# Attention beside an MLP on one core: where the products of softmax weights and values stand in the order of TensorE's work

## The chip, the core and the metric

The kernel runs on one core of a Trainium2 chip. The metric is the device time of one launch in microseconds (us), the median of three runs. The profile is one execution of the same program, recorded on the chip.

## The reference

```python
scores = (1 / sqrt(64)) * q @ k.T              # 8 batches, 8 heads, 576 positions, head size 64
scores = where(pos_q // 64 >= pos_k // 64, scores, -1e9)
attn   = softmax(scores)                       # less the row's maximum; the sum gets 1e-9 added
x      = attn @ v                              # heads side by side: x is 4608 x 512
out    = (sigmoid(x @ w_gate) * (x @ w_val)) @ w_out     # 512 -> 1536 -> 512
```

All of it is float32 at the outside.

## The kernel before

**Two halves.** The first half, about 550 us of the span, is the attention with a part of the MLP dealt in between. The second half is the rest of the MLP (lines 875 and 953), and the change does not reach its code. Where an operand is split into a high and a low fp32r part (names in H and L, such as `KH`, `KL`), a product is three matmuls: high by high, high by low, low by high.

**Pairs.** The attention goes over 32 pairs `p` of heads, four to a batch. Of a pair's 576 query rows, 512 are four blocks of 128 (3, 2, 1, 0); the last 64 rows of both heads are the tail. The steps of a pair, as the tables name them:

- `s`: scores of blocks 3, then 2, then 1 and 0 together (`s_blocks`, line 258, `bank<-KH,QH` and the like; block 0 is `bank<-KQ`). Per block VectorE masks (L409, L411), takes the maxima (L385), and ScalarE takes the exponentials into `P` (L388). The two heads lie in the upper and lower 64 rows of TensorE (64\*128).
- `t`: scores of the tail (`s_tail`; `QBH`, `QBL`), 128\*128; maxima L425, exponentials `Pt` L427.
- `r`: reciprocals of the row sums (L433 to L436), then two DMAs on SP's queue: to DRAM (`r_d`, L439) and back, spread over the partitions (`rb`, L442).
- `tr3`, `tr2`, `trl`, `trt`: transposes of the weights of block 3, block 2, blocks 1 and 0, and the tail, on TensorE (L262, `bank<-ident,P` and `bank<-ident,Pt`); ScalarE copies each result from PSUM into `G1` or `G0` (L363). The copy of `trt` (`128x8x64` and `128x2x64` in the order) puts the tail's columns beside those of the blocks in `G1`.
- `AV`: products of weights and values (`av`, `bank<-G,VS`, 128\*64: the heads lie in the left and right 64 columns). Its first matmul reads 320 columns of `G1`, the tail's 64 among them. VectorE multiplies the result by `rb` into `xT` (L507), ScalarE and GpSimd split `xT` for the MLP (L514, L519).
- `k`, `q`: the next pair's operands are prepared (VectorE transposes L290, casts L327, L328, L331, L332, GpSimd L336), and loads are issued on SP's queue.

**Order.** A table names the steps of a pair in their order with a number behind each: so many ticks, and in each tick some products of the MLP are dealt (`m`, lines 131 and 138: 128 by 512, full array). Pairs 0 to 7 have their own tables (`ALONE`, `FIRST`, `TURN`); pairs 8 to 31 use `REST`. `AV` in the row of pair p is that of pair p-1. A scheduler puts the instructions on the engines' queues; `behind(a, b)` keeps `a` behind `b`. In pairs 8 to 31 the first matmul of `s` and that of `AV` stand behind the product dealt last, and the last matmul of either is put into `hold`, behind which products dealt later and the transposes stand. A product may be dealt up to three ticks ahead of its place. A batch's MLP products are added to the supply with the `AV` of its last pair.

**PSUM.** The attention has three double banks in turn (`two_banks`, names `bank`), the MLP two single ones (`mbank`, names `m`). A step that takes a double bank waits until its last use has been read.

Of the kernel before, what the change touches and what calls it, by code (L numbers as in the profile page):

```python
# [30 lines left out]
         ("tr3", 1), ("r", 0), ("ld", 0))  # L31
ALONE = (("S3", 1), ("TR2", 1), ("k", 1), ("S2", 1), ("q", 1), ("m3", 0), ("m2", 0), ("TRt", 1), ("t", 1), ("TRl", 1), ("sl", 1), ("AV", 2),
         ("tr3", 1), ("r", 0), ("ld", 0))
REST = (("s", 3), ("t", 1), ("AV", 2), ("tr3", 1), ("r", 0), ("k", 0), ("tr2", 1), ("q", 0), ("trl", 2), ("trt", 2))
TURN = (("s3", 1), ("TR2", 1), ("k", 0), ("s2", 1), ("TRt", 1), ("q", 0), ("t", 1), ("TRl", 1), ("sl", 1), ("AV", 1),
        ("tr3", 1), ("r", 0), ("tr2", 1), ("trl", 1), ("trt", 1))
N_FIRST = 7
# [5 lines left out]
def attn_glu_kernel(ctx: ExitStack, tc: tile.TileContext, q, k, v, w_gate, w_val, w_out, out):  # L43
# [26 lines left out]
    def behind(ins, other):  # L70

        tc.add_manual_dep(ins, other.name, mybir.DependencyInfo(mybir.DependencyClass.NoSync,
                                                                mybir.DependencyReason.DATA), reason="order")
# [90 lines left out]
    with ExitStack() as s2:  # L164
# [78 lines left out]
        pe_last, first_mm, hold, dealt, chain = [], [], [], [], []  # L243
# [23 lines left out]
        def two_banks():  # L267
            return ps_a.tile([P, 2, 512], F32, name="bank")
# [80 lines left out]
        def attend(p):  # L349
# [10 lines left out]
            rest = p > N_FIRST  # L360
# [4 lines left out]
            def scores(ps, i, c):  # L365


                n = P * (i + 1)
                q = slice(i * P, (i + 1) * P)
                ops = [(KQ[:, 1, q], KQ[:, 0, :n])]  # L370
                if rest and i:
                    q = slice((i - 1) * P, i * P)
                    ops = [(QS[a][:, q], KS[b][:, :n]) for a, b in ((0, 0), (1, 0), (0, 1))]
                for k, (x, y) in enumerate(ops):
                    for h in range(2):
                        matmul(ps[:, h, c:c + n], lhsT=x[rows(h)], rhs=y[rows(h)], start=(k == 0),
                               stop=(k == len(ops) - 1), tile_position=(64 * h, 0))
                        if h == k == 0:
                            first_mm[:] = pe_last

            def softmax(ps, i, c):
                n = P * (i + 1)
                c0 = col[i]
                Pi = keep[i] = p_tile(i)
                mark("DVE", nc.vector.tensor_reduce(out=nm[:, c0:c0 + 2], in_=ps[:, :, c:c + n], axis=AX.X, op=ALU.max,  # L385
                                                    negate=True))
                for h in range(2):
                    mark("ACT", nc.scalar.activation(out=Pi[:, h], in_=ps[:, h, c:c + n], func=AF.Exp,  # L388
                                                     bias=nm[:, c0 + h:c0 + h + 1], accum_out=sm[:, 5 * h + i:5 * h + i + 1]))
                    if i == 3 and 0 < p < NP:  # L390
                        behind(last["ACT"], q_copied[-1])

            def s_blocks(*groups, alone=False):


                tiles = [two_banks() for _ in groups]
                for k, (ps, group) in enumerate(zip(tiles, groups)):
                    for j, i in enumerate(group):
                        scores(ps, i, 2 * P * j)
                        if rest and dealt and k == j == 0:  # L400
                            behind(first_mm[0], dealt[-1])
                if rest:
                    hold[:] = pe_last
                if alone:
                    yield
                for ps, group in zip(tiles, groups):
                    n = P * (group[0] + 1)
                    if len(group) == 1:
                        nc.vector.memset(ps[0:64, :, n - 64:n], -1e9)  # L409
                    else:  # L410
                        nc.vector.memset(ps[0:64, :, P:3 * P].rearrange("p h (i n) -> p h i n", i=2)[:, :, :, 64:], -1e9)  # L411
                    for j, i in enumerate(group):
                        softmax(ps, i, 2 * P * j)
# [109 lines left out]
            def step(what):  # L523
                if what in ("S3", "S2"):
                    soft[what] = s_blocks((int(what[1]),), alone=True)
                    next(soft[what])
                elif what in ("m3", "m2"):
                    run(soft.pop("S" + what[1]))
                elif what == "s":
                    run(s_blocks((3,), (2,), (1, 0)))  # L530
                elif what[0] == "s":
                    run(s_blocks({"s3": (3,), "s2": (2,), "sl": (1, 0)}[what]))
                elif what == "t":
                    s_tail()
                elif what == "r":
                    recip()
                elif what == "tr3":
                    tr_main(3)
                elif what == "tr2":
                    tr_main(2)  # L540
                elif what == "trl":
                    tr_low()
                elif what == "trt":
                    tr_tail()
                else:
                    av()
                    finish()
# [264 lines left out]
        for p in range(n + 1):  # L812
# [3 lines left out]
            tick = 0  # L816
            for what, places in (ALONE if p < NP else FIRST if p < N_FIRST else TURN if p == N_FIRST else REST):
                if what.startswith(("AV", "TR")):
# [17 lines left out]
                for _ in range(places if now else 6 if what == "AV" else 0):  # L836
                    pe_ticks.append(pe_last[0])
                    acc += rate
                    while acc >= 1:
                        acc -= 1  # L840
                        left -= 1
                        ins = next(mlp, None)
# [252 lines left out]
```

## Time and profile before

| | |
|---|---|
| median of 3 runs | 1180.55 us (1180.47 to 1180.87) |
| span of the profiled execution | 1177.6 us |
| TensorE (PE) busy | 1153.6 us, 98% |
| weight loads (PEld) | 976.3 us, 83% |
| VectorE (DVE) / ScalarE (ACT) / GpSimd (POOL) | 776.6 / 617.4 / 349.6 us |
| granted TensorE clock, mean | 0.995 |
| first scores of pair 8 / 13 / 31 | 125.67 / 220.17 / 527.61 us into the span |

The profile's page gives the span alone for its execution and no device time of its own; the median of the runs lies 2.95 us above that span. PE is TensorE's matmuls, PEld its weight loads. In a row of the timeline stand the start, the duration, the engine, the line, the operation with its output and inputs, and the count of instructions that were merged; the ends of matmuls are modelled and overlap the next one's start, so the step from start to start is what a matmul costs.

### The profile page before, as it was taken

How to read it: one execution, taken by the hardware profiler on the slowest of the kernel's cores; microseconds unless marked ns; L12 is line 12 of the kernel's file. 1: busy time of each engine (PE TensorE's matmuls, PEld its weight loads, DVE VectorE, ACT ScalarE, POOL GpSimd, SP SyncE). 2: the span in 40 equal slices, each digit the busy share in tenths (PEclk: the TensorE clock that was granted, in tenths of full speed). 3: DMA queues.
4: the chain of work that ended last, by engine and by line, in shares of the span. 5: the costliest groups of instructions: out<-in, count | busy, mean ns of one | idle time of the engine just before them, and what ended most of it. 6: DMA issues, size and time to landing. Idle time of an engine off the chain costs nothing.

```text
span 1177.6 us, 19283 instructions
## 1 busy us (share of the span) xinstructions
PE 1153.6 (98%) x6749; PEld 976.3 (83%) x6749; DVE 776.6 (66%) x1405; ACT 617.4 (52%) x1364; POOL 349.6 (30%) x390
## 2 busy tenths in 40 slices
PE   6999999999999999999999999999999999999998
PEld 4555778778777877787889899999999998998997
DVE  5778845454564555457959977867877746746754
ACT  5867766766676676666334443553453422423421
POOL 2345523222331322234002133032033263262330
PEclk8999999999999999999999999999999999999999
DMA  8765434435434443534323236235197455164241
GB/s 198 180 144 115 104 89 100 117 74 127 99 89 112 102 122 71 125 105 134 111 95 126 91 120 223 71 136 202 39 339 276 158 172 179 39 212 132 83 143 54
DMA packets 253361, 153.34 MB, mean 130 GB/s; under 512 B 193232, under 2 KB 215248, under 8 KB 252624
## 3 DMA queue, kind: packets, MB, share of 16 engines
q1 hardware_dynamic: 241600, 132.15, 40.1%
q10 hardware_dynamic: 11280, 18.91, 4.4%
q8 instruction: 53, 0.87, 0.3%
q0 software_dynamic: 384, 1.05, 0.3%
q14 instruction: 44, 0.36, 0.1%
HBM read 104.73 MB, written 47.33 MB: 129 GB/s over the span
## 4 chain that ended last, share of the span: by engine, by line
PE 90%; DVE 5%; ACT 2%; issue 1%; DMA 1%; POOL 0%; SPq 0%; DVEq 0%; ACTq 0%
PE b L875 27%; PE bank L258 14%; PE m L131 14%; PE m L953 11%; PE m L138 7%; PE bank L262 6%; PE b L953 5%; PE bank L131 3%; ACT P L388 1%; PE m L262 1%; PE bank L138 1%; DVE nm L385 1%; DVE XL L765 0%; DMA raw<-in_moe_w_out_dram 0%; DMA rqk<-in_k_dram 0%
## 5 line engine op out<-in xcount | busy, mean ns | idle before, releaser
L875 PE MATMUL b<-XH,w 128*128 128x384 f32 x1344 | 349.2, 335 | 1.2 <-DVE g L921 1.2
L875 PEld LDWEIGHTS b<-XH,w 128*128 128x128 f32 x1344 | 243.9, 188 | 5.2 <-DVE g L921 1.6
L875 PE MATMUL b<-XL,w 128*128 128x384 f32 x672 | 223.5, 335 | 0.0
L388 ACT ACTIVATE P<-bank,nm 128x512 f32<-128x512 f32 (+3 forms) x256 | 132.1, 530 | 68.3 <-DVE nm L385 68.2
L385 DVE TENSOR_REDUCE nm<-bank 128x2 f32<-128x1024 f32 (+3 forms) x128 | 105.4, 823 | 40.7 <-ACT P L388 37.6
L875 PEld LDWEIGHTS b<-XL,w 128*128 128x128 f32 x672 | 126.1, 188 | 1.6
L953 PE MATMUL m<-wo,hH 128*128 128x512 f32 x384 | 125.0, 391 | 0.0
L363 ACT COPY G<-bank 128x768 f32<-128x768 f32 (+3 forms) x140 | 93.2, 694 | 26.2 <-PE bank L262 25.3
L258 PE MATMUL bank<-G,VS 128*64 128x320 f32 (+4 forms) x896 | 93.9, 360 | 0.1
L751 POOL TENSOR_TENSOR XB<-XB 128x384 f32<-128x384 f32 x20 | 20.7, 1037 | 237.9 <-DMA XB<-xT_d 191.6
L138 PE MATMUL m<-wo,hH 128*128 128x512 f32 x256 | 85.4, 398 | 1.4 <-ACT ost L632 1.0
L258 PEld LDWEIGHTS bank<-G,VS 128*64 128x64 f32 x896 | 55.9, 137 | 36.7 <-issue 4.3
L900 ACT ACTIVATE g<-g 128x384 f32<-128x384 f32 x72 | 37.8, 526 | 88.5 <-DVE g L913 48.6
L953 PEld LDWEIGHTS m<-wo,hH 128*128 128x128 f32 x384 | 72.0, 188 | 13.5
L131 PE MATMUL m<-XH,wv 128*128 128x512 f32 x240 | 82.3, 400 | 0.0
L131 PE MATMUL m<-XH,wg 128*128 128x512 f32 x240 | 82.1, 399 | 0.0
L764 ACT CAST XH<-XB 128x1536 fp32r<-128x1536 f32 (+2 forms) x72 | 65.2, 941 | 29.4 <-DVE XB L762 24.1
L765 DVE TENSOR_TENSOR XL<-XB,XH 128x1536 fp32r<-128x1536 f32 (+2 forms) x72 | 75.8, 1084 | 0.0
L262 PEld LDWEIGHTS bank<-ident,P 128*128 128x128 f32 x560 | 65.8, 141 | 11.5 <-ACT P L388 0.8
L953 PE MATMUL m<-wo,hL 128*128 128x512 f32 x192 | 75.2, 392 | 0.0
L262 PE MATMUL bank<-ident,P 128*128 128x128 f32 x560 | 74.8, 273 | 0.1
L409 DVE MEMSET bank<- 64x128 f32 x64 | 10.6, 165 | 88.0 <-PE bank L258 87.3
(183 smaller groups left out, 2339.5 us busy)
## 6 DMA issues: line engine op xcount, KB each, us to landing
xT_d<-xT ACTq DMA_DIRECT2D x32, 288.0 KB
XB<-xT_d SPq DMA_DIRECT2D x16, 576.0 KB
part_d<-ost SPq DMA_DIRECT2D x36, 256.0 KB
VS<-in_v_dram SPq DMA_DIRECT2D x64, 128.0 KB
part_d<-ost ACTq DMA_DIRECT2D x32, 256.0 KB
rqk<-in_k_dram SPq DMA_DIRECT2D x108, 72.0 KB
rqk<-in_q_dram SPq DMA_DIRECT2D x108, 72.0 KB
wgv_d<-st SPq DMA_DIRECT2D x8, 896.0 KB
```

Of the source, the lines that this page charges most:

```text
L131: mm = nc.tensor.matmul(ps, lhsT=lh, rhs=rh, start=(i == 0), stop=(i == n - 1))
L138: mm = nc.tensor.matmul(ps, lhsT=lh[:, f, t * P:(t + 1) * P], rhs=rh, start=(f == i == 0), stop=(f == F1 - 1 and i == 2))
L258: pe_last[:] = [nc.tensor.matmul(*args, **kw).ins]
L262: pe_last[:] = [nc.tensor.transpose(*args).ins]
L363: mark("ACT", nc.scalar.copy(out=dst, in_=src))
L385: mark("DVE", nc.vector.tensor_reduce(out=nm[:, c0:c0 + 2], in_=ps[:, :, c:c + n], axis=AX.X, op=ALU.max, negate=True))
L388: mark("ACT", nc.scalar.activation(out=Pi[:, h], in_=ps[:, h, c:c + n], func=AF.Exp, bias=nm[:, c0 + h:c0 + h + 1], accum_out=sm[:, 5 * h ...
L764: nc.scalar.copy(out=XO[j][0][:, a:b], in_=x)
L765: sub = nc.vector.tensor_sub(out=XO[j][1][:, a:b], in0=x, in1=XO[j][0][:, a:b].bitcast(F32))
L875: mm = nc.tensor.matmul(ps, lhsT=lh, rhs=rh, start=(first and k == 0), stop=(k == n - 1), skip_group_check=not first)
L900: mark2("ACT", nc.scalar.activation(out=t, in_=c, func=AF.Tanh, scale=0.5))
L953: mm = nc.tensor.matmul(po[t], lhsT=lh[:, f, t * P:(t + 1) * P], rhs=rh, start=(half == 0 and i == 0), stop=(half == 1 and i == 5))
```

## The change

In `REST` the products of weights and values move from behind the tail's scores to the head of the row, with no tick between them and the scores of the pair. The ticks move too: four behind the scores instead of three, two behind the tail's scores instead of one, one behind `trl` instead of two, three behind `trt` instead of two; there are twelve as before. With `AV` the point at which a batch's products join the supply moves to the head of the pair. The first matmul of the scores is kept behind the product dealt last and behind `hold`, which is the last matmul of `AV` there.

```diff
-REST = (("s", 3), ("t", 1), ("AV", 2), ("tr3", 1), ("r", 0), ("k", 0), ("tr2", 1), ("q", 0), ("trl", 2), ("trt", 2))
+REST = (("AV", 0), ("s", 4), ("t", 2), ("tr3", 1), ("r", 0), ("k", 0), ("tr2", 1), ("q", 0), ("trl", 1), ("trt", 3))
...
                         scores(ps, i, 2 * P * j)
-                        if rest and dealt and k == j == 0:
-                            behind(first_mm[0], dealt[-1])
+                        if rest and k == j == 0:
+                            for ins in (*dealt, *hold):
+                                behind(first_mm[0], ins)
```

What this does to the queues is seen in the order of the built programs. In it `bank<-ident,Pt` are the tail's transposes, `bank<-G,VS` is `AV`, `bank<-KH,QH` the scores, `m<-` the MLP's products. A line number behind the diff is one higher after the change.

TensorE before, at the seam between two pairs (the end of pair 15, the start of pair 16):

```order
L131 MATMUL m<-XH_387,wv_113 128x512
L262 MATMUL bank<-ident,Pt 128x128 x5
L138 MATMUL m<-wo,hH 128x512
L138 MATMUL m<-wo,hL 128x512
L138 MATMUL m<-wo,hH 128x512 x2
L258 MATMUL bank<-KH,QH 128x512 x2
L258 MATMUL bank<-KH,QL 128x512 x2
```

Four products stand between the tail's transposes and the next scores.

TensorE before, in pair 16, where the tail's scores (`QBH`, `QBL`) end and `AV` of pair 15 stands:

```order
L258 MATMUL bank<-KL,QBH 128x288
L258 MATMUL bank<-G_2842,VS_94 64x320 x6
L258 MATMUL bank<-G_2842,VS_94 64x64 x2
L258 MATMUL bank<-G_2842,VS_94 64x192 x2
L258 MATMUL bank<-G_2843,VS_94 64x256 x2
L258 MATMUL bank<-G_2843,VS_94 64x128 x2
L138 MATMUL m<-wo,hL 128x512
```

`AV` stands between the tail's scores and MLP products, far behind the transposes that it reads.

TensorE now, at the same seam, between pairs 15 and 16:

```order
L138 MATMUL m<-wo,hH 128x512 x2
L138 MATMUL m<-wo,hL 128x512
L138 MATMUL m<-wo,hH 128x512
L262 MATMUL bank<-ident,Pt 128x128 x5
L258 MATMUL bank<-G_2861,VS_94 64x320 x6
L258 MATMUL bank<-G_2861,VS_94 64x64 x2
L258 MATMUL bank<-G_2861,VS_94 64x192 x2
L258 MATMUL bank<-G_2862,VS_94 64x256 x2
L258 MATMUL bank<-G_2862,VS_94 64x128 x2
L258 MATMUL bank<-KH,QH 128x512 x2
```

The tail's transposes, `AV` of the same pair and the scores of the next now stand one behind the other without a product between them.

ScalarE now, at the seam between pairs 19 and 20 (`G_3638` is the copy of `trl`, the two rows of `G_3637` that of `trt`, `ost` an MLP output):

```order
L328 ACTIVATE QH<-KQ 128x448
L363 COPY G_3638<-bank 128x768
L633 ACTIVATE ost<-m 128x512
L363 COPY G_3637<-bank 128x8x64
L363 COPY G_3637<-bank 128x2x64
L636 DMA part_d<-ost 128x512
L515 CAST XH_387<-xT 128x576
```

ScalarE copies the low blocks, then an MLP output, then the tail; the cast of `xT` (L515) now stands behind the tail's copies, ahead of the next pair's exponentials.

In full the order of TensorE's steps in a pair was `s` (20 matmuls), 12 products, `t`, `AV`, 6 products, `tr3`, 3, `tr2`, 3, `trl`, 8, `trt`, 4. Now it is `AV`, `s`, 20 products, `t`, `tr3`, 4, `tr2`, 9, `trl`, 3, `trt` (in every fourth pair 7 and 5 instead of 9 and 3). The seams behind pairs 8 to 11 still have 5 to 11 products between `trt` and `AV`; the 20 seams behind pairs 12 to 31 have none. Behind the last pair's `AV` follow 311 products instead of 323.

## The prediction

> **What bounds the kernel now.** I read the page first, then the stretch of the attention, then TensorE's timeline through one seam between two pairs.
>
> ```profile
> span 1177.6 us, 19283 instructions
> PE 1153.6 (98%) x6749; PEld 976.3 (83%) x6749; DVE 776.6 (66%) x1405; ACT 617.4 (52%) x1364; POOL 349.6 (30%) x390
> PE   6999999999999999999999999999999999999998
> PEclk8999999999999999999999999999999999999999
> ```
>
> ```profile
> core 0: us, PE busy (x) PEld busy (x) DVE busy (x) ACT busy (x) POOL busy (x), PEclk, DMA share, GB/s
> 220.17:527.61 307.44, 307.44 (x2108) 244.00 (x2107) 164.59 (x324) 209.47 (x522) 87.91 (x126) 1.00 0.44 103
> ```
>
> TensorE sets the time. From the first scores of pair 13 (220.17 us) to those of pair 31 (527.61) it is busy for 307.44 of 307.44 us at clock 1.00: 18 pairs of 17.08 us. Nothing waits there that costs anything, so the change can gain only what TensorE loses between matmuls of unlike kinds, and any new wait of TensorE is a loss in full. The timeline from the end of pair 15 into pair 16, TensorE alone:
>
> ```profile
> 269.85 0.71 PE L262 MATMUL bank<-ident,Pt 128*128 128x128 f32 x5
> 270.31 0.47 PE L138 MATMUL m<-wo,hH 128*128 128x512 f32 x1
> 270.63 0.39 PE L138 MATMUL m<-wo,hL 128*128 128x512 f32 x1
> 270.85 0.63 PE L138 MATMUL m<-wo,hH 128*128 128x512 f32 x2
> 271.41 0.50 PE L258 MATMUL bank<-KH,QH 64*128 64x512 f32 x2
> ...
> 272.74 0.28 PE L258 MATMUL bank<-KH,QH 64*128 64x256 f32 x2
> ...
> 273.41 0.50 PE L138 MATMUL m<-wo,hL 128*128 128x512 f32 x1
> 273.74 0.63 PE L138 MATMUL m<-wo,hH 128*128 128x512 f32 x2
> 274.20 0.40 PE L138 MATMUL m<-wo,hL 128*128 128x512 f32 x1
> ...
> 276.29 0.29 PE L258 MATMUL bank<-KH,QBH 128*128 128x288 f32 x1
> ...
> 277.16 2.93 PE L258 MATMUL bank<-G,VS 128*64 128x320 f32 x28
> 280.02 0.50 PE L138 MATMUL m<-wo,hL 128*128 128x512 f32 x1
> 280.36 0.63 PE L138 MATMUL m<-wo,hH 128*128 128x512 f32 x2
> ```
>
> A product among its like costs 0.23 us (273.74 to 274.20 for two). Between kinds a step is longer: the scores start at 271.41, where two products from 270.85 on end at 271.31, so 0.10 late; the first product behind AV takes 0.34 instead of 0.23 (280.02 to 280.36); the first behind the tail's transposes 0.32 (270.31 to 270.63). These are the gaps that a regrouping can close.
>
> **The seam now: a new wait.** The order shows that at the 20 seams behind pairs 12 to 31 AV follows its own tail's transposes at once. AV's first matmul reads what ScalarE copies from those transposes. Before, four products lay between and, except at the last seam, the next scores, 12 products and the tail's scores as well. ScalarE at the same place, the forms of that copy, and a place of the first 60 us where TensorE waited for ScalarE:
>
> ```profile
> 270.60 0.75 ACT L363 COPY G<-bank 128x512 f32<-128x512 f32 x2 [1.60 <-PE bank L262]
> L363 ACT COPY G<-bank 128x512 f32<-128x512 f32 x28 | 16.4, 587 | 18.8 <-PE bank L262 18.8
> 51.85 0.60 ACT L300 ACTIVATE KQ<-m 128x512 f32<-128x512 f32 x1 [0.85 <-PE m L262]
> 52.50 0.66 PE L262 MATMUL m<-ident,Pt 128*128 128x128 f32 x4 [0.58 <-ACT KQ L300]
> ```
>
> ScalarE had idled 1.60 us and began the copy at 270.60, when the transposes were through. The first of its two parts, 128x512, takes 0.587 and ends at 271.19. TensorE goes on 0.05 us after ScalarE's end (51.85 + 0.60 = 52.45, then 52.50): 271.24. Without the wait AV could start at 270.31, where the next product stood, plus 0.10 for the change of kind: 270.41. So 0.83 us of nothing at each such seam. The second part ends 0.2 us later and is read by AV's fourth pair of matmuls, over a microsecond in: hidden.
>
> ScalarE must also be free in time. From the end of the low blocks' transposes to the end of the tail's stand three products and five transposes, 0.79 + 0.46 = 1.25 us.
>
> ```profile
> L363 ACT COPY G<-bank 128x768 f32<-128x768 f32 x56 | 44.1, 801 | 6.6 <-PE bank L262 5.8
> L155 ACT CAST hH<-h 128x512 fp32r<-128x512 f32 x36 | 22.6, 627 | 32.0 <-DVE h L150 32.0
> ```
>
> The low blocks' copy takes 0.80: through in time. In every fourth pair the cast `hH` (0.63) stands behind it, 1.43 in all less the 0.1 by which such instructions overlap: about 0.1 late, 0.03 on the mean. Where `ost` stands there, five products precede and cover it. Term: 20 x 0.86 = +17.2 us. Its ends: 0.78 a seam, with the hand-over of 0.05 hidden, and 1.1, if an extra ScalarE instruction of 0.6 stands uncovered at half the seams.
>
> **Fewer changes of kind.** Before, a pair had four: products to scores, scores to products, tail's scores to AV, AV to products. Now it has three: transposes to AV, AV to scores, scores to products. Tail's scores to transposes is none (both 128\*128; 276.29 follows its product at the usual step). The price of one comes from the last pair, where AV is split by products:
>
> ```profile
> 544.69 1.84 PE L258 MATMUL bank<-G,VS 128*64 128x320 f32 x12
> 546.45 0.50 PE L131 MATMUL bank<-XH,wg 128*128 128x512 f32 x1
> ...
> 548.41 0.40 PE L131 MATMUL bank<-XH,wg 128*128 128x512 f32 x1
> 548.74 1.31 PE L258 MATMUL bank<-G,VS 128*64 128x64 f32 x16
> 549.98 0.50 PE L138 MATMUL m<-wo,hL 128*128 128x512 f32 x1
> ```
>
> Split, AV takes 1.76 + 1.24 = 3.00 us; whole, 2.86 (277.16 to 280.02). With 0.10 ahead (548.41 + 0.23 to 548.74) and 0.11 behind, one further visit, two changes, costs 0.35: 0.17 for one. Besides, a pair now goes from transposes to products three times instead of four, 0.09 each. Together 0.26 a pair, in 24 pairs -6.2 us. The change from AV to scores shows nowhere; I take it at 0.17 like the others, the nearest rows. If it costs nothing, 0.43 a pair is saved (-10.3); if it costs two changes, 0.09 (-2.2).
>
> The Trainium skill, TensorEngine Tiling (Array Packing), Key Properties, says that changing the tiling mode drains TensorE. By that rule transposes to products, one mode, would cost nothing; the row of 270.31 says 0.09. By the rule alone the saving would be 24 x 0.17 = 4.1 and the sum 2 us higher; I keep the row.
>
> **What hides the rest.** The xT multiplications stand in VectorE's queue ahead of the next maxima, and the scores of blocks 1 and 0 take the PSUM that AV held:
>
> ```profile
> 281.62 0.78 DVE L507 TENSOR_TENSOR xT<-bank,rb 128x320 f32<-128x320 f32 x2
> 262.34 0.19 ACT L427 ACTIVATION_READ_ACCUMULATOR Pt<-bank,nm 128x1 f32 x1
> 265.78 1.75 SPq L442 DMA_DIRECT2D rb<-r_d  x3
> 283.90 1.77 SPq L442 DMA_DIRECT2D rb<-r_d  x3
> 138.56 1.74 SPq L442 DMA_DIRECT2D rb<-r_d  x3
> 142.96 1.42 POOL L156 TENSOR_TENSOR hL<-h,hH 128x512 fp32r<-128x512 f32 x1 [0.81 <-DMA rb<-r_d]
> ```
>
> Those scores start 1.33 us behind the first (272.74 - 271.41); the multiplications are through some 1.0 after AV (0.78 and two hand-overs). Covered by 0.3, if `rb` has landed. `rb` is issued until 13.2 us after the pair's first scores (265.78 + 1.75 - 254.33, one pair earlier than 271.41) and in the slower case until 14.3 (283.90 + 1.77 - 271.41); it lands 2.7 later (138.56 + 1.74 to 142.96): 15.9, or 17.0. The tail's scores now stand behind 20 products instead of 12, 1.85 us later; its exponentials, until now held by ScalarE's queue (262.34 is 8.0 after the scores), move by about 1.4. So `rb` is there at 17.3, or 18.4, and is wanted at about 17.9. About a quarter of the seams may be late, by some 0.2 beyond the cover: +1.0 in all, between 0 and +6.
>
> The DMAs of the step keep their order on SP's queue; the V loads, which waited there for AV, wait less. The next pair's operands (`KH` to `QL`) are prepared as late as the tail's exponentials and have over 4 us left. The run of 20 products crosses chains of 12, each 2.8 us in one of two banks; ScalarE's `tanh` and `ost` must come between exponentials of 0.7. Nothing, since a bank is wanted again only 2.8 us later; at most a wait as in this row, 1.0 at one seam in four, +5:
>
> ```profile
> PE m L138 <- ACT ost L632: 1.0, 1, 1.0
> ```
>
> The 12 products that leave the end for the pairs cost 0.23 on both sides: nothing. The second half is the same.
>
> **The sum.** +17.2 - 6.2 + 1.0 = +12.0. The profiled execution's span becomes 1177.6 + 12.0 = 1189.6; the median lies 2.95 above the span: 1192.5.
>
> **Rivals.**
> - *The gaps win (faster).* If AV's wait were covered, the saved changes alone would give 1180.55 - 6.2 = 1174.3. It decides at a stall of 0.31 us (6.2 / 20). Against it stands the copy: 0.587 of ScalarE's work can't lie beside anything, since no product stands there. 0.03.
> - *No change.* The stall would have to be 0.2 to 0.43: the copy half as long, or part of AV ahead of it. The same row speaks against it. 0.04.
> - *`rb` becomes the bound (slower still).* If it lands 2 us later than worked out, at 19.3 against 17.9 and the cover of 0.3, the scores of blocks 1 and 0 wait 1.1: 20 x 1.1 = +22 on the sum, 1214. It decides from 0.9 us later on. For it: the margin is that small. Against it: every us of stall elsewhere gives it a us more. 0.06.
> - *The run of 20 products starves on its PSUM banks.* +5 and more, with the stall at its upper end: 1197 to 1204. 0.11.
>
> **How the numbers follow.** The forecast has 0.76, between 20 x 0.78 - 10.3 = +5 (1185) and 20 x 1.1 - 2.2 = +20 (1200). With the starving banks the range goes to 1204. What a measurement here can tell from no change is about 0.2%, 2.4 us. Faster 0.03, same 0.04, slower 0.93.
>
> **What would show it.** Right: in the pairs from 12 on TensorE idles 0.8 to 0.9 us ahead of AV, released by ScalarE's `G`, some 17 us in all; the step from pair to pair grows from 17.08 to about 17.7; the pairs ahead of 12 grow by nothing. Wrong: a pair of 17.0 or less; idle time ahead of `KH,QH` 64x256 released by VectorE's `xT` (then `rb`); idle time ahead of `m` inside the run of 20; or a lower granted clock.

## The result, and the profile after

The changed kernel takes 1196.47 us (median of 4 runs, 1195.20 to 1196.68) against 1180.51 beside it: 16.0 us slower, a ratio of 1.014 (1.0126 to 1.0154). The profiled execution took 1196.68 us with a span of 1194.8, so 1.9 us lie around the span. Its page, to hold against the rows of before:

```profile
span 1194.8 us, 19185 instructions
PE 1152.6 (96%) x6749; PEld 981.1 (82%) x6749; DVE 779.3 (65%) x1405; ACT 618.9 (52%) x1364; POOL 343.4 (29%) x390
PE   7899899999999999999999999999999999999998
PEclk8999899999999999999999999999999999999999
```

The span grew by 17.2 us and TensorE's busy time did not: the loss is in the main TensorE standing still. In the slice of the clock that begins at 119 us there is now an 8. The waits of TensorE's matmuls on `bank` (engine, waiting line, releaser: us in total, times, longest):

```profile
PE bank L258 <- ACT G L363: 15.4, 21, 1.9
PE bank L258 <- DVE xT L508: 5.0, 2, 3.8
```

One seam, between pairs 17 and 18, in TensorE's timeline, and ScalarE there:

```profile
297.14 0.63 PE L131 MATMUL m<-XH,wg 128*128 128x512 f32 x2
297.61 0.71 PE L262 MATMUL bank<-ident,Pt 128*128 128x128 f32 x5
298.99 2.93 PE L258 MATMUL bank<-G,VS 128*64 128x320 f32 x28 [0.68 <-ACT G L363]
301.85 0.50 PE L258 MATMUL bank<-KH,QH 64*128 64x512 f32 x2
```

```profile
298.36 0.75 ACT L363 COPY G<-bank 128x512 f32<-128x512 f32 x2 [0.31 <-PE bank L262]
```

The tail's transposes begin at 297.61, ScalarE starts its copy at 298.36 as they are through, and AV begins at 298.99, just behind the copy's first part. From the first scores of pair 13 (231.43) to those of pair 31 (549.85) there are 18 pairs. Seventeen of them are 17.59 to 17.62 us long, before 17.08; one, pair 24, has 19.12.

The first seam, between pairs 7 and 8, and the one other with a wait for `xT`:

```profile
127.23 2.93 PE L258 MATMUL bank<-G,VS 128*64 128x320 f32 x28 [1.88 <-ACT G L363]
...
135.38 0.58 PE L258 MATMUL bank<-KH,QH 64*128 64x256 f32 x2 [3.79 <-DVE xT L508]
```

```profile
427.84 0.39 PE L258 MATMUL bank<-KH,QH 64*128 64x256 f32 x2 [1.25 <-DVE xT L508]
```

ScalarE, SyncE's queue and VectorE at the first seam:

```profile
125.37 0.62 ACT L122 CAST wo<-XB 128x512 fp32r<-128x512 f32 x1
125.89 1.45 ACT L363 COPY G<-bank 128x768 f32<-128x768 f32 x3
129.41 2.12 SPq L443 DMA_DIRECT2D rb<-r_d  x3
134.07 0.49 DVE L508 TENSOR_TENSOR xT<-bank,rb 128x320 f32<-128x320 f32 x1 [3.49 <-DMA rb<-r_d]
```

And three stretches around it (length; busy time of each engine; granted clock, DMA share, GB/s):

```profile
127.00:136.00 9.00, 4.98 (x46) 3.44 (x48) 3.73 (x8) 1.72 (x4) 1.75 (x3) 0.91 0.34 101
136.00:141.20 5.20, 5.20 (x19) 4.01 (x18) 4.61 (x9) 3.96 (x13) 3.81 (x3) 0.50 0.15 58
141.20:145.00 3.80, 3.80 (x22) 3.28 (x21) 1.95 (x5) 1.49 (x7) 0.00 (x0) 1.00 0.00 0
```

`AV` of pair 7 waits 1.88 us for the tail's copy, which stands behind a cast of `wo` and the low blocks' copy on ScalarE. The scores of blocks 1 and 0 of pair 8 wait 3.79 us for the PSUM that VectorE hasn't read, since `rb` isn't there before 134.07. And then TensorE runs at half its clock: the same view gives 1.00 from 131.50 to 134.40 us and 0.50 from 134.40 to 141.20, of which 5.8 us lie behind the wait. Pair 7's own row, `TURN`, puts the reciprocals near its end, and its `AV` used to stand 8 us later.

### The profile page after: what moved, and what is told of

The parts are those of the page before. It is cut to its first block, busy times and chain, and to the rows that moved or that the text cites. A ratio compares the mean times of both kernels' runs of the same rounds, so it can differ in the third digit from the quotient of the medians.

```text
span 1194.8 us, 19185 instructions
## 1 busy us (share of the span) xinstructions
PE 1152.6 (96%) x6749; PEld 981.1 (82%) x6749; DVE 779.3 (65%) x1405; ACT 618.9 (52%) x1364; POOL 343.4 (29%) x390
## 4 chain that ended last, share of the span: by engine, by line
PE 85%; DVE 4%; ACT 4%; DMA 3%; issue 2%; SPq 2%; POOL 0%; DVEq 0%; ACTq 0%
PE b L876 29%; PE m L131 13%; PE bank L258 12%; PE m L954 11%; PE m L138 7%; PE b L954 5%; PE bank L262 5%; PE bank L131 3%; ACT G L363 2%; ACT P L388 1%; PE bank L138 1%; DMA r_d<-rT 1%; DMA rb<-r_d 1%; SPq L239 1%; DMA rqk<-in_k_dram 1%
## 5 line engine op out<-in xcount | busy, mean ns | idle before, releaser
L508 DVE TENSOR_TENSOR xT<-bank,rb 128x320 f32<-128x320 f32 x64 | 26.4, 453 | 119.4 <-PE bank L258 98.5
L520 POOL TENSOR_TENSOR XL<-xT,XH 128x576 fp32r<-128x576 f32 x32 | 46.6, 1457 | 163.7 <-ACT XH L515 163.7
```

Of the source, the lines that this page charges most:

```text
L520: nc.gpsimd.tensor_sub(out=XL[:, hp], in0=xT, in1=XH[:, hp].bitcast(F32))
```

## The experiments

The theory: TensorE waits at each seam for ScalarE's copy of the tail, `rb` comes next, and fewer changes of kind give a part back. The rivals were that the grouping or the moved ticks cost by themselves, and that the waits come from VectorE's queue, not from `rb`. The kernel before took 1179.64 to 1179.72 us beside these runs.

**Half of the copy's cover, from AV itself.** In `av` the products that read `G0` go first:

```diff
-for i, (G, pieces) in enumerate(((G1, G1P), (G0, G0P))):
+for i, G, pieces in ((1, G0, G0P), (0, G1, G1P)):
```

> The changed kernel, with AV's loop turned round: the products of blocks 1 and 0 (they read G0, the copy of trl) stand ahead of those that read G1 and with it the tail's copy. Nothing else moves. Theory (the loss is TensorE's wait for the tail's copy, 0.82 us at 20 seams): the G0 part is 384 of 640 columns of a piece that took 1.24 us, so about 0.74 us of AV lies beside the copy, the wait falls to about 0.1, and the time from 1196.5 to about 1182; pairs of 16.9 us. Rival (the loss comes from standing AV and scores together, drains or queues, and the wait only sits where the time is lost): no change, 1196, with the idle time in another place.

Measured: 1189.04 us, ratio 1.0083 (1.0055 to 1.011), with runs from 1186 to 1194. Its seam and its waits:

```profile
243.04 0.71 PE L262 MATMUL bank<-ident,Pt 128*128 128x128 f32 x5
243.68 3.02 PE L258 MATMUL bank<-G,VS 128*64 128x256 f32 x28
246.63 0.50 PE L258 MATMUL bank<-KH,QH 64*128 64x512 f32 x2
```

```profile
PE bank L258 <- DVE xT L508: 9.0, 7, 3.8
PE bank L258 <- ACT G L363: 1.4, 1, 1.4
```

From the transposes to AV it is 0.64 us instead of 1.38, AV takes 2.95 instead of 2.86, and most pairs without a wait take about 16.98. The copy's wait has gone, as expected, but the time is 7 us above the expectation: `xT` now holds TensorE 7 times. So where the seam gets shorter `rb` is late; that it is `rb` and not something else of VectorE's is shown by the run with `rb` taken away, below.

**Without the first seam.** Pair 8 keeps the old row:

```diff
-TURN if p == N_FIRST else REST):
+TURN if p == N_FIRST else REST8 if p == N_FIRST + 1 else REST):     # REST8: REST of the kernel before
```

> The changed kernel, but pair 8 keeps the row of the kernel before, so that AV of pair 7 stands behind the tail's scores of pair 8. Theory (the seam behind pair 7, which the prediction did not count, costs 1.9 us for the copy, 3.8 us for rb and some 2 us of lowered clock): about 1189, no wait of TensorE for xT at pair 8, granted clock there 1.0. Rival (the waits only move on to the seam behind pair 8, since rb of any pair in that stretch is late): 1195 to 1197.

Measured: 1189.55 us, 1.0083 (1.0068 to 1.0098), no wait for `xT` at pair 8 (one of 0.8 us is left, at pair 24), clock 1.00 from 125 to 145 us, most later pairs 17.59 to 17.62. With pair 8's old row 7 of the 16 us are gone. Not all of that is the first seam: two of the 20 later seams (behind pairs 13 and 14) no longer wait for the copy in this kernel, 0.7 us each, and the seam behind pair 8 waits 0.9 for it.

**Products between the transposes and AV.** At the end of `tr_tail`, so that products dealt later stay behind it:

```diff
                 transpose(pt[1][:, :P], Pt[:, S - P:S], ident)
+                if rest:
+                    hold[:] = pe_last
```

> The changed kernel, but products dealt behind the tail's transposes are kept behind them, so that nine stand between those transposes and AV at the seams. Theory: no wait for the copy (20 x 0.82 us less), while the saving from fewer changes of kind stays: pairs of 16.8 us, 1180 with the seam behind pair 7 as it is. If rb is the next bound (it lands about 17.3 us behind the scores and is wanted at 17.0 then), 0.2 to 1 us of waits for xT at each seam come in its place: 1184 to 1196. Rival (grouping itself costs): pairs of 17.1 or more without any wait.

Measured: 1196.02 us (1192 to 1201), 1.0141 (1.0112 to 1.017). With both edits, this one and pair 8's old row:

> Both edits: pair 8 with the row of before, and products kept between the tail's transposes and AV. Theory: 1173 to 1174, faster than the kernel before by the 0.28 us a pair that fewer changes of kind save (23 x 0.28 = 6.4 us). If rb is the next bound: 1177 to 1188. Rival (fewer changes of kind save nothing): 1180 or more with pairs of 17.08 and no waits.

Measured: 1189.86 us (1186 to 1192), 1.0092 (1.0075 to 1.0109). Nine or ten products now stand at each of the 20 seams, and yet nothing was won. TensorE's waits in the first of the two and in the second (whose lines are one higher), and VectorE's in the second:

```profile
PE bank L258 <- DVE xT L510: 12.5, 12, 3.4
```

```profile
PE bank L259 <- DVE xT L511: 7.1, 10, 1.4
...
DVE xT L511 <- DMA rb<-r_d: 42.1, 10, 5.3
```

Pairs of 36 products without such a wait take 16.86 to 16.95, so the wait for the copy is gone at the 20 seams and the grouping costs nothing; what came in their place is `rb`. The branch of the expectation with `rb` as the next bound holds, and it took nearly all of the gain.

**`rb` taken away.** The last kernel, but from pair 9 on `xT` is multiplied by the `rb` of the pair before:

```diff
-in1=rb[:, q0:q0 + n]
+in1=rb_used[:, q0:q0 + n]          # rb_used: rb of pair p-1
```

> Pair 8 with the row of before and products kept between the tail's transposes and AV, and in pairs 9 to 31 VectorE multiplies AV's result by the rb of the pair before instead of its own, which has long landed; all DMAs and instructions stay. This leaves the right normalization out. Theory (rb is the wait that is left in that kernel): no wait of TensorE for xT, pairs of 16.85 us, about 1174, below the kernel before, with runs that agree again within 1 us. Rival (the waits come from VectorE's queue or from the PSUM bank, whatever rb does): 1186 to 1190, as without this edit.

Measured: 1176.18 us (1175.81 to 1177.28), 0.9974 (0.9963 to 0.9985): 13.7 us less than with its own `rb`, no wait for `xT`, and the runs agree again. Scores of pairs 17 and 31:

```profile
292.04 0.50 PE L259 MATMUL bank<-KH,QH 64*128 64x512 f32 x2
...
528.22 0.50 PE L259 MATMUL bank<-KH,QH 64*128 64x512 f32 x2
```

That is 16.87 us a pair over 14 pairs. The rival that VectorE's queue or the PSUM does it falls, and so does the one that the moved ticks cost by themselves in these pairs: they are the changed kernel's ticks, 4 and 2.

**The tail's scores sooner.** With nine products at the seam and pair 8's old row, ticks 2 and 4 instead of 4 and 2 (fifteen products ahead of the tail's scores instead of twenty):

> Pair 8 with the row of before, products kept between the tail's transposes and AV, and the ticks behind the scores and the tail's scores 2 and 4 instead of 4 and 2: fifteen products instead of twenty ahead of the tail's scores, so rb is issued about 1.1 us sooner. Theory (rb is late by 0.2 to 1.4 us at a part of the seams): waits for xT fall from 7 to 12 us to 0 to 3, 1175 to 1180. Rival (how late the tail's scores stand doesn't matter, ScalarE's queue or the DMA's own time sets rb): 1185 to 1190.

Measured: 1180.74 us (1178.94 to 1182.96), 1.0009 (0.9999 to 1.0018); no wait for `xT`, pairs of 16.88. In the attention it is as fast as the one with the old `rb`. The 4.6 us between their medians lie outside it. The profiled execution here was the slowest of ten, with a span 7.1 us above the other's: 2.1 of them lie ahead of pair 8, 4.9 behind the first scores of pair 31. There TensorE waits for MLP work on VectorE, and the clock is 0.50 for some 3.4 us behind the longest of these waits (586.5 to 589.9), 0.98 on the mean of the stretch:

```profile
PE m L139 <- DVE h L151: 2.6, 1, 2.6
...
540.00:640.00 100.00, 96.66 (x455) 79.55 (x454) 80.97 (x150) 38.16 (x60) 13.87 (x14) 0.98 0.33 107
```

Why `h` is later here than with the old `rb` (a wait of 0.7) wasn't tried.

**The low blocks first, and the tail sooner.** `G0` first, pair 8's old row, ticks 2 and 4:

> Pair 8 with the row of before, AV's products of blocks 1 and 0 first, and ticks 2 and 4 as in the run with the tail sooner; products are not kept behind the tail's transposes, so one to three stand there. Theory: copy covered by 0.74 us of AV's own work and 0.23 to 0.7 of products, rb sooner: pairs of 16.9 us, 1175 to 1180. Rival: as before this edit, 1183 to 1189.

Measured: 1175.60 us (1173.56 to 1176.02), 0.9963 (0.9950 to 0.9976), with the right normalization: the fastest, 4.1 us under the kernel before. Its seam, and the scores of pair 31:

```profile
286.28 0.71 PE L263 MATMUL bank<-ident,Pt 128*128 128x128 f32 x5
286.74 0.48 PE L132 MATMUL m<-XL,wg 128*128 128x512 f32 x1
287.06 0.63 PE L132 MATMUL m<-XH,wg 128*128 128x512 f32 x2
287.62 2.93 PE L259 MATMUL bank<-G,VS 128*64 128x256 f32 x28
290.47 0.50 PE L259 MATMUL bank<-KH,QH 64*128 64x512 f32 x2
...
526.97 0.50 PE L259 MATMUL bank<-KH,QH 64*128 64x512 f32 x2
```

Pairs of 16.89 us ((526.97 - 290.47) / 14), no wait. The same with ticks 4 and 2 parts its two edits:

> Pair 8 with the row of before and AV's products of blocks 1 and 0 first, but with the changed kernel's ticks 4 and 2, so that the tail's scores stand behind twenty products again. It parts the two edits of the fastest run. Theory (with the copy covered, rb is what the ticks decide): pairs of 16.98 broken by waits for xT of 3 to 8 us in all, 1180 to 1186. Rival (the low blocks first is all it takes): 1175 to 1177.

Measured: 1183.51 us, 1.0038 (1.0024 to 1.0052), with 3.8 us of waits for `xT` at 5 seams. The ticks are worth 8 us, and they do two things. They decide whether `rb` is in time: besides the 3.8 us of waits the clock is 0.50 from 415.7 to 419.1 us, behind the longest of them. And with ticks 2 and 4 one to three products stand at most seams, where with 4 and 2 none do: pairs without a wait take 16.96 to 17.00 here and 16.88 to 16.91 there. The two weren't parted.

**The ticks alone.** The kernel before with the ticks 4, 2, 1, 3, and `("AV", 0)` still behind `t`:

> The kernel before with the new ticks (4, 2, 1, 3) and AV left behind the tail's scores, with no tick of its own. Theory (all of the loss comes from AV's new place): 1180 to 1183, the upper end because in every fourth pair AV is split by products, at 0.35 us a split; no wait for the tail's copy. Rival (the run of 15 to 20 products behind the scores or the later tail's scores cost by themselves): 1185 or more.

Measured: 1188.95 us, 1.0080 (1.0065 to 1.0095), and the expectation was wrong: the time lies where the rival had it, that the moved ticks cost by themselves. There is no wait for the tail's copy or `xT` at the seams, and unsplit pairs take 17.02 to 17.06, so the run of products costs nothing in them. Two things cost. In five pairs AV is split twice by products, and such a pair takes 17.74, which is 0.7 more: 3.5 in all. And ahead of 150 us the MLP's products overtake the conversion of `w_out`, for a long wait, behind which the clock halves:

```profile
147.68 0.79 PE L138 MATMUL m<-wo,hH 128*128 128x512 f32 x1 [4.15 <-ACT wo L122]
```

```profile
150.00:153.00 3.00, 3.00 (x21) 2.60 (x18) 2.27 (x4) 0.82 (x3) 0.00 (x0) 0.50 0.00 0
```

A wait of 1.5 us for `h` at 591 us comes on top. The changed kernel splits AV once (behind pair 11) besides the last pair's, which every kernel here splits, and never waits for `wo`, so this is hardly a share of its loss; but with `AV` behind `t` the ticks aren't free, and this run doesn't part them from the move of AV as cleanly as meant.

**The changed kernel without the wait for `rb`.** The old `rb` from pair 7 on, nothing else:

> The changed kernel with one edit: from pair 7 on VectorE multiplies AV's result by the rb of the pair before, which has landed; all instructions and DMAs stay, the right normalization is left out. Theory (of the 17 us of the change, 1.9 at the seam behind pair 7 and 14.5 at the 20 later seams are the copy, 5.0 are rb, and 2.6 are the clock that falls to half behind the 3.8 us wait for rb): no wait for xT, clock 1.0 at pair 8, the wait of 1.9 for the copy there as before, pairs of 17.6: 1189. Rival (the clock falls for the copy's wait or for the change of kind, not for rb's): a clock of 0.5 at pair 8 all the same, 1191 to 1192.

Measured: 1190.02 us, 1.0088 (1.0073 to 1.0103). Its waits and the clock behind the first seam:

```profile
PE bank L258 <- ACT G L367: 15.5, 21, 1.9
...
PE bank L258 <- DVE xT L512: 0.2, 1, 0.2
```

```profile
131.00:145.00 14.00, 13.79 (x88) 11.41 (x85) 12.18 (x24) 9.55 (x25) 7.48 (x6) 1.00 0.24 64
```

The copy's waits are all there, 1.9 at the first seam among them, and the clock stays at 1.00: without the wait for `rb` it isn't halved. From pair 8's first scores to pair 9's it is 19.62 us here, with the same products, and 25.89 in the changed kernel: wait and clock are 6.3 us of the change, 3.8 the wait and 2.5 the clock. The whole kernel is 6.4 us faster, though the late `rb` of pair 24 is gone as well; in this profile pair 8 begins 1.3 us later, and why stays open.

## Why the prediction was right, and where its terms were off

The way, the main mechanism and the range held; the time was 4 us above the forecast of 1192.5. That it came so near is in part luck: the terms that were summed came out 2.5 us too high, and a seam that wasn't counted cost 8.2. By its terms:

| term | predicted | measured |
|---|---|---|
| tail's copy at 20 seams | +17.2 | +14.4 |
| fewer changes of kind | -6.2 | -4.6 |
| `rb` at later seams | +1.0 | +1.5 |
| the seam behind pair 7 | none | +8.2 |
| waits of before that went (1.0, 0.4, 0.3, 0.2) | none | -1.9 |
| sum, against the span's +17.2 | +12.0 | +17.6 |

The copy is 20 times 0.72 and the saving 24 times 0.19, both read from pairs of 36 products; `rb` is pair 24's 19.12 less 17.6.

- *The seam was rightly found, and 0.09 of it wrongly booked.* From the transposes' start to AV it is 1.38 us, of which the prediction took 0.46 for five transposes and 0.10 for the change of kind: 0.82, against its 0.83. But pairs of 17.605 against the 16.89 of the kernel without the stall say 0.72. The difference is the 0.09 that the prediction charged to going from transposes to products. The rows of before that it had not laid side by side:

```profile
264.43 1.04 PE L262 MATMUL bank<-ident,P 128*128 128x128 f32 x8
265.22 0.47 PE L131 MATMUL m<-XL,wg 128*128 128x512 f32 x1
...
266.00 0.82 PE L262 MATMUL bank<-ident,P 128*128 128x128 f32 x6
266.57 0.47 PE L131 MATMUL m<-XL,wv 128*128 128x512 f32 x1
```

  Eight transposes take 0.79 to the next start, six 0.57, five 0.46: 0.11 each, and 0.09 short. By this reading the late first product is the end of the last transpose. So a stall counted from 0.46 is 0.09 too long, and a pair with one such passage less saves nothing: two kernels with two and with four passages a pair take 16.88 and 16.89.
- *The saving is 0.19 a pair,* 17.08 less 16.89, where the prediction took 0.26. Its price of one change, 0.17, was near. By the rule that it had set against the row (the Trainium skill, TensorEngine Tiling (Array Packing), Key Properties: a change of tiling mode drains TensorE) only the changes count, and the runs agree with it. At the 20 seams the stall is 0.09 too long and the saving 0.09 too large, and the two cancel. The 0.03 a seam for ScalarE's casts did not come either: every fourth pair is no longer than the others.
- *`rb` was the narrow thing that the prediction said,* but the size of the term is luck: about five seams late by 0.2 were forecast, and one came, between pairs 24 and 25, with a wait of 1.25 and a pair 1.5 longer. There the two loads that SyncE's queue issues just ahead of `rb` take about 1 us more than at pair 23, and `rb` is issued that much later:

```profile
401.46 0.88 SPq L239 DMA_DIRECT2D rqk<-in_k_dram  x2
419.21 1.84 SPq L239 DMA_DIRECT2D rqk<-in_k_dram  x2
```

  The same two take 2.00 to 2.29 us at pair 24 in the kernels with `G0` first, with products between and with pair 8's old row, and 0.88 in the kernel before. Why they do stays open.
- *The seam behind pair 7 was missed.* The order was read from pair 8's row on, and the 20 seams were counted where `REST` stands on both sides. But `AV` of pair 7 moves as well, behind a pair with another table, whose reciprocals come late: 1.9 for the copy, 3.8 for `rb`, and a halved clock that cost 2.5. A lower clock and a wait ahead of `KH,QH` 64x256 were two of the signs by which the prediction was to be known wrong, and both came: the step that failed is the count of the seams. It gave the clock no price, and the wait one for the later seams alone (1.0, up to 6).
- *The starving banks* did not come: no wait ahead of `m` in the run of 20.
- *The gaps win* was dismissed for this change and is true beside it: with the copy covered and `rb` in time, the kernel with three changes of kind instead of four is 4.1 us faster, 0.37%; 0.19 a pair in the 23 pairs with the new row would be 4.4.

## What to carry to other kernels

Where a step is moved to follow its producer directly, the cover that it had is the price: count the time from the producer's end through the copy to the consumer's start, then ask what the shorter way makes late next; here each repair of the first wait ran into the second until that was given time too. Count every place where the moved step lands, the joints to other tables first. A price read from one late start should be held against groups of other sizes before it is booked.

## What the runs showed of the hardware

Waits of TensorE of 3.38, 3.77, 3.79 and 4.15 us (products between, `G0` first, the changed kernel, the ticks alone) were followed by some 3 to 6 us at a granted clock of 0.50; waits of 1.88 and 0.7 were not. In the changed kernel this cost 2.5 us beyond the wait's own length. The Trainium skill, TensorE: Matmul & The Clock Gate, What's actually happening, has half rate after an idle window of about 3.4 us; three of these four runs agree, in which the clock fell 3.5 to 3.8 us after the wait began. In the changed kernel it fell 2.8 us after (131.59 to 134.40), and shorter waits don't fit: those of 1.76, 2.02 and 2.60 us (`G0` first with ticks 4 and 2, `G0` first, the tail's scores sooner) were followed by about 3.4 us at 0.50 as well, and one of 3.00 in the run with pair 8's old row was not. Of these the one of 1.76 and the one of 3.00, each with the stretch behind it:

```profile
414.85 0.38 PE L259 MATMUL bank<-KH,QH 64*128 64x256 f32 x2 [1.76 <-DVE xT L509]
415.70:419.00 3.30, 3.30 (x8) 2.62 (x9) 2.53 (x5) 2.76 (x9) 1.28 (x1) 0.50 0.64 162
...
21.55 0.66 PE L263 MATMUL m<-ident,rqk 128*128 128x128 f32 x4 [3.00 <-ACT G L364]
21.60:30.00 8.40, 7.47 (x50) 4.64 (x52) 6.75 (x15) 6.58 (x19) 2.94 (x4) 1.00 0.72 197
```

So the length of one wait alone doesn't say whether the clock falls; what else decides it wasn't tried.
